# Attention with one query block per head: K of two pairs in 8 KB rows, K and V loaded 64 partitions at a time

## The chip, the cores and the metric

One core of a Trainium2 chip runs the kernel. The metric is device time in microseconds (us); lower is better. A run is called slow when it lies over 1.5% above the fastest of the same kernel.

## The reference

16 batches, 32 query heads, 8 KV heads, 16 queries per head, 2048 keys, head size 128, all in bfloat16. Four query heads share one KV head, so each of the 128 KV heads has 64 query rows.

```python
k = jnp.repeat(k, rep, axis=1); v = jnp.repeat(v, rep, axis=1)      # rep = 4
scores = jnp.einsum("bhqd,bhkd->bhqk", q, k) * D ** -0.5
p = _softmax(scores, axis=-1)
return jnp.einsum("bhqk,bhkd->bhqd", p, v)
```

K and V are 67.1 MB each and are read once. Q and the output are 2.1 MB each.

## The kernel before

A *pair* is two neighbouring KV heads: 128 query rows, one per partition of the scores. The loads fill buffers in SBUF; their rows, 128 here, are called partitions. A load is cut into pieces, here one per partition and row: the prediction calls them descriptors, the trace shows them as packets (32,768 of 4 KB before, 128 for each of the 256 loads of K and V). SyncE (SP) issues all loads and stores in one fixed order, with rings of buffers. Each K or V load is one head, 512 KB, as 128 partitions with 4 KB (16 keys) each:

```python
NBK = 10; NBV = 14; DV = 2; DSTORE = 5          # buffers; V follows K by two pairs, stores by five
...
if kind == "K":
    dst, src = Kn[s][:, :].bitcast(BF16), kf[x].rearrange("(a j) d -> a (j d)", j=J)      # J = 16
elif kind == "V":
    dst, src = Vb[s][:, :, :], vf[x].rearrange("(a j) d -> a j d", j=J)
...
sp.dma_start(dst, src).then_inc(prog.sem_dma[kind][s], 16)
```

VectorE (DVE) transposes K, 1238 ns for a head. TensorE (PE) makes the scores S of a pair (128 by 2048, in PSUM). ScalarE (ACT) takes the exponential, writing P with its columns in another order and summing the rows. PE transposes P, DVE or ACT copies the result out of PSUM, PE multiplies with V, and the result is divided by the row sum and stored:

```python
ins = eng.activation(P[p % 2][:, :].rearrange("m (r a j) -> m a r j", a=4, j=32),
                     src[:, :].rearrange("m (a r j) -> m a r j", a=4, j=32), ACT.Exp, ...,
                     accum_out=rowsum[:, p:p + 1])
```

A second program in the same kernel, with a maximum taken off first, runs only when row sums leave a safe range; with these inputs it does not run.

Of the kernel before, what the change touches and what calls it, by code (L numbers as in the profile page):

```python
# [12 lines left out]
NBK = 10  # L13
NBV = 14
# [3 lines left out]
DV = 2  # L18
# [4 lines left out]
HINT = {"pe": 7, "dve": 10, "act": 3, "pool": 1, "sp": 6}  # L23
# [4 lines left out]
    ("dve", "kx"): 1.25, ("dve", "mx"): 2.38, ("dve", "rc"): 0.17, ("dve", "nm"): 0.36,  # L28
    ("dve", "pe"): 0.69, ("act", "pe"): 1.03, ("act", "qe"): 1.06, ("dve", "qe"): 1.25, ("act", "nm"): 0.42,
    ("act", "ex"): 2.22, ("pool", "qr"): 1.6, ("act", "qr"): 1.1, ("dve", "qr"): 1.1,  # L30
# [6 lines left out]
_SIZE = {"K": 0.524, "V": 0.524, "Q": 0.27, "ST": 0.06}  # L37
_ISSUE = 0.5
_T0 = 1.0
_ENGS = {"kx": ("dve",), "mx": ("dve",), "rc": ("dve",), "nm": ("act", "dve"), "pe": ("act", "dve"),  # L40
         "qe": ("act", "dve"), "qr": ("pool",), "ex": ("act",), "qt": ("pe",), "S": ("pe",), "pt": ("pe",), "pv": ("pe",)}
_PRIO = {"S": 0, "mx": 0, "ex": 0, "pt": 1, "pe": 1, "pv": 2, "rc": 2, "nm": 2, "kx": 3, "qr": 3, "qt": 3, "qe": 3}


def make_ops(NP, pairs_per_chunk, general):

    deps = {}
    dma = []
    ch = lambda p: p // pairs_per_chunk
    n_ch = ch(NP - 1) + 1  # L50
    last_of = lambda c: min(NP, (c + 1) * pairs_per_chunk) - 1

    def add(op, *d):
        deps[op] = [x for x in d if x is not None]

    opt = lambda ok, op: op if ok else None
    for c in range(n_ch):
        add(("Q", c), *[opt(c >= 2, ("qr", c - 2, x)) for x in range(4)])
        for x in range(4):
            prev = ("qe", c, x - 1) if x else opt(c >= 1, ("qe", c - 1, 3))  # L60
            add(("qr", c, x), ("Q", c), opt(c >= 1, ("qt", c - 1, x)))
            add(("qt", c, x), ("qr", c, x), prev)
            add(("qe", c, x), ("qt", c, x), opt(c >= 2, ("S", last_of(c - 2))))
    for g in range(2 * NP):
        p = g // 2
        add(("K", g), opt(g >= NBK, ("kx", g - NBK)))
        add(("V", g), opt(g >= NBV, ("pv", (g - NBV) // 2)))
        add(("kx", g), ("K", g), opt(p >= NKT, ("S", p - NKT)))
    for p in range(NP):
        add(("S", p), ("kx", 2 * p), ("kx", 2 * p + 1), *[("qe", ch(p), x) for x in range(4)],  # L70
            opt(p >= 1, ("mx" if general else "ex", p - 1)))
        if general:
            add(("mx", p), ("S", p), opt(p >= 2, ("ex", p - 2)))
        add(("ex", p), ("mx" if general else "S", p), *[opt(p >= 2, ("pt", p - 2, h)) for h in range(2)])
        for h in range(2):
            add(("pt", p, h), ("ex", p), opt(p >= 1, ("pe", p - 1, h)))
            add(("pe", p, h), ("pt", p, h), opt(p >= NPT, ("pv", p - NPT)))
        add(("pv", p), ("pe", p, 0), ("pe", p, 1), ("V", 2 * p), ("V", 2 * p + 1), opt(p >= 1, ("nm", p - 1)))
        add(("rc", p), ("ex", p))
        add(("nm", p), ("pv", p), ("rc", p), opt(p >= NBO, ("ST", p - NBO)))  # L80
        add(("ST", p), ("nm", p))
    qstep = {max(0, c * pairs_per_chunk - QLEAD): c for c in range(n_ch)}
    dma.append(("Q", 0))
    for t in range(NP + max(DV, DSTORE) + 1):
        if t < NP:
            dma += [("K", 2 * t), ("K", 2 * t + 1)]
        if qstep.get(t, 0):
            dma.append(("Q", qstep[t]))
        if 0 <= t - DV < NP:
            dma += [("V", 2 * (t - DV)), ("V", 2 * (t - DV) + 1)]  # L90
        if 0 <= t - DSTORE < NP:
            dma.append(("ST", t - DSTORE))
    return deps, dma


def pair_of(op, pairs_per_chunk):
    if op[0] in ("qr", "qt", "qe"):
        return op[1] * pairs_per_chunk - 1.5
    return op[1] // 2 if op[0] == "kx" else op[1] + {"S": -1.5, "pv": 1.5}.get(op[0], 0)


def build_schedule(NP, pairs_per_chunk, general):

    deps, dma = make_ops(NP, pairs_per_chunk, general)
    left = sorted((op for op in deps if op[0] in _ENGS),
                  key=lambda op: (pair_of(op, pairs_per_chunk), _PRIO[op[0]]))
    done, free = {}, {"pe": _T0, "dve": _T0, "act": _T0, "pool": _T0, "sp": _T0}
    progs = {"pe": [], "dve": [], "act": [], "pool": [], "sp": []}
    dma_left, dma_end = list(dma), _T0 + _DMA_LAT

    def ready(op):
        r = 0.0
        for d in deps[op]:
            if d not in done:
                return None
            r = max(r, done[d])
        return r

    while left or dma_left:
        best = None  # L120
        if dma_left:
            rd = ready(dma_left[0])
            if rd is not None:
                st = max(free["sp"] + _LAT_SAME, rd + _LAT)
                best = ((round(st, 3), -1, -1), st, "sp", dma_left[0])
        seen = 0
        for op in left:
            rd = ready(op)
            if rd is None:
                continue  # L130
            dur = lambda e: _DUR[op[0]] if e == "pe" else _DUR[(e, op[0])]
            engs = ("dve", "act") if op[:2] == ("qr", 0) else _ENGS[op[0]]
            fin = min((max(free[e] + _LAT_SAME, rd + _LAT) + dur(e), e) for e in engs)
            st = fin[0] - dur(fin[1])
            cand = ((round(st, 3), pair_of(op, pairs_per_chunk), _PRIO[op[0]]), st, fin[1], op)
            if best is None or cand[0] < best[0]:
                best = cand
            seen += 1
            if seen > 40:
                break  # L140
        _, st, eng, op = best
        if eng == "sp":
            dma_left.pop(0)
            end = st + _ISSUE
            dma_end = max(dma_end, end + _DMA_LAT) + _SIZE[op[0]] / _BW
            done[op] = dma_end + (_V_LATE if op[0] == "V" else 0.0)
        else:
            left.remove(op)
            end = st + (_DUR[op[0]] if eng == "pe" else _DUR[(eng, op[0])])
            done[op] = end  # L150
        free[eng] = end
        progs[eng].append(op)
    return deps, progs, max(done.values())


def bass_standalone__gqa_softmax__sampling_kernel(
# [28 lines left out]
    Kn = [sb(f"Kn{i}", [128, J * 64], I32) for i in range(NBK)]  # L185
    KT = [sb(f"KT{i}", [128, 2, J * 64], I32) for i in range(NKT)]
    Vb = [sb(f"Vb{i}", [128, J, 128], BF16) for i in range(NBV)]
    Sneg = [sb(f"Sneg{i}", [128, Sk], F32) for i in range(2)]
# [3 lines left out]
    nbias = sb("nbias", [128, NP], F32)  # L192
    rowsum = sb("rowsum", [128, NP], F32)
    ones = sb("ones", [128, 1], F32)
# [13 lines left out]
    rings = {"K": NBK, "V": NBV, "Q": 2, "ST": NBO}  # L208

    class Program:  # L210
        def __init__(self, tag, general):
            self.general = general
            self.deps, self.progs, _ = build_schedule(NP, qch // 128, general)
            self.sem_eng = {e: sem(f"{tag}_{e}") for e in ("pe", "dve", "act", "pool")}
            self.sem_dma = {kind: [sem(f"{tag}_{kind}{i}") for i in range(n)] for kind, n in rings.items()}
            self.where = {op: (e, i + 1) for e in self.sem_eng for i, op in enumerate(self.progs[e])}

        def point(self, op):
            if op[0] in rings:
                n = rings[op[0]]  # L220
                return self.sem_dma[op[0]][op[1] % n], 16 * (op[1] // n + 1)
# [36 lines left out]
    def elementwise(eng, me, prog, before_last=None):  # L258
        waits = prog.waiter(eng, me)
        for op in prog.progs[me]:  # L260
# [5 lines left out]
            if kind == "kx":  # L266
                ins = eng.transpose(KT[(p // 2) % NKT][:, p % 2, :], Kn[p % NBK][:, :])  # L267
# [5 lines left out]
            elif kind == "mx":  # L273
                ins = eng.tensor_scalar(Sneg[p % 2][:, :], S_ps[:, :], -scale, None,
                                        op0=ALU.mult, op1=ALU.min, accum_out=nbias[:, p:p + 1])
            elif kind == "ex":
                src = Sneg[p % 2] if prog.general else S_ps
                ins = eng.activation(  # L278
                    P[p % 2][:, :].rearrange("m (r a j) -> m a r j", a=4, j=32),
                    src[:, :].rearrange("m (a r j) -> m a r j", a=4, j=32), ACT.Exp,  # L280
                    bias=nbias[:, p:p + 1] if prog.general else 0.0, scale=-1.0 if prog.general else scale,
                    accum_out=rowsum[:, p:p + 1])
# [19 lines left out]
    def transfers(sp, prog):  # L302
        waits = prog.waiter(sp, "sp")
        for op in prog.progs["sp"]:
# [3 lines left out]
            s = x % rings[kind]  # L308
            if kind == "K":
                dst, src = Kn[s][:, :].bitcast(BF16), kf[x].rearrange("(a j) d -> a (j d)", j=J)  # L310
            elif kind == "V":
                dst, src = Vb[s][:, :, :], vf[x].rearrange("(a j) d -> a j d", j=J)
# [6 lines left out]
    def matmuls(pe, prog):  # L319
        waits = prog.waiter(pe, "pe")  # L320
        for op in prog.progs["pe"]:
# [11 lines left out]
            elif kind == "S":  # L333
                c, pp = divmod(p, qch // 128)
                for x in range(4):
                    for a in range(4):
                        for gg in range(2):
# [14 lines left out]
            else:  # L352
                for r in range(J):
                    for gg in range(2):
# [3 lines left out]
                            Vb[(2 * p + gg) % NBV][:, r, :],  # L358
# [20 lines left out]
    with nc.Block() as block:  # L379
# [30 lines left out]
        def _(dve):  # L410
            def count_within():
                dve.wait_ge(*fast.point(("ex", NP - 1)))
# [41 lines left out]
```

## Time and profile before

| | before |
|---|---|
| median (range) | 356.46 us (356.08 to 356.99) |
| span of the profiled run | 353.4 us |
| busy: PE, DVE, ACT | 66%, 68%, 55% |
| bytes moved in the queue of the loads | 138.43 MB |
| rate in the steady part | about 410 GB/s |

The first fence is from the page of the kernel before. The first two rows cut the span into 40 slices: the busy share of the 16 DMA engines in tenths, and the rate in GB/s. Then come the packet count, the chain of work that ended last (shares of the span), DVE's largest group (busy us, mean ns | idle us before it and what ended that), and the two large groups of DMA issues (KB each, median us from issue to landing).

```profile
DMA  7999999999999999999999999999999999999971
GB/s 276 414 408 408 413 408 407 412 413 406 413 408 410 412 410 412 408 413 411 410 411 411 408 412 413 395 411 413 409 411 409 406 413 410 403 409 405 411 287 42
DMA packets 47288, 139.24 MB, mean 394 GB/s; under 512 B 13440, under 2 KB 13440, under 8 KB 47232
DMA 54%; PE 16%; DVE 14%; ACT 7%; SPq 5%; issue 4%
...
L267 DVE STREAM_TRANSPOSE KT<-Kn 128x1024 int32<-128x1024 int32 x128 | 158.1, 1238 | 75.7 <-DMA Kn<-in_k_dram 74.6
...
Kn<-in_k_dram SPq DMA_DIRECT2D x128, 512.0 KB, 12.1
Vb<-in_v_dram SPq DMA_DIRECT2D x128, 512.0 KB, 13.3
```

The DMA engines are full in nearly every slice at about 410 GB/s, and no compute engine is above 68%. DVE's idle time is mostly waiting for K. So the loads bound this kernel, and 138.4 MB at 410 GB/s make 338 of the 353 us.

The end is the other part. These are stretches of the span (start:end and length in us, busy us with instruction counts for PE, its weight loads, DVE, ACT and POOL, then PE clock, DMA share, GB/s).

```profile
330.00:335.00 5.00, 2.77 (x74) 2.07 (x53) 3.02 (x4) 1.97 (x2) 0.00 (x0) 1.00 1.02 409
335.00:340.00 5.00, 3.40 (x102) 2.29 (x104) 4.11 (x7) 3.36 (x4) 0.00 (x0) 1.00 0.94 355
340.00:345.00 5.00, 3.89 (x96) 2.91 (x80) 2.90 (x6) 1.97 (x2) 0.00 (x0) 1.00 0.59 232
```

The rate falls off from 335 us on, while the last loads are still to come.

### The profile page before, as it was taken

The page shows a single profiled execution, that of the slowest core. Times are in us where ns is not written, and L with a number is a line of the kernel's source. Part 1 is how long each engine was busy: PE and PEld are TensorE (multiplying, and loading weights), DVE is VectorE, ACT ScalarE, POOL GpSimd, SP SyncE. Part 2 cuts the span into 40 slices and gives each one's busy share as a digit, 9 for nine tenths or more (in the row PEclk, how much of TensorE's full clock was granted, in tenths as well). Part 3 has the DMA queues.
Part 4 walks back from the last instruction along what each step waited for, and adds up shares of the span by engine and source line. Part 5 has one row for each costly group of instructions (what it writes and reads, how often), then busy time and mean ns, then how long its engine had stood idle before and what let it go on. Part 6 is the DMA issues. An engine that isn't in the chain of part 4 may idle for free.

```text
span 353.4 us, 11937 instructions
## 1 busy us (share of the span) xinstructions
PE 233.8 (66%) x5378; PEld 167.9 (48%) x5378; DVE 239.4 (68%) x340; ACT 193.8 (55%) x214; POOL 28.9 (8%) x35
## 2 busy tenths in 40 slices
PE   2499765776666857756556876676656677566663
PEld 1266543554444634544444655454444545444442
DVE  4668786787685666766766676675776647866761
ACT  6458555754347646665456753576554755554450
POOL 1040000300012000310004000040000400000000
PEclk9999999989999998999999988999999989999997
DMA  7999999999999999999999999999999999999971
GB/s 276 414 408 408 413 408 407 412 413 406 413 408 410 412 410 412 408 413 411 410 411 411 408 412 413 395 411 413 409 411 409 406 413 410 403 409 405 411 287 42
DMA packets 47288, 139.24 MB, mean 394 GB/s; under 512 B 13440, under 2 KB 13440, under 8 KB 47232
## 3 DMA queue, kind: packets, MB, share of 16 engines
q1 hardware_dynamic: 47232, 138.43, 98.7%
q8 instruction: 43, 0.70, 0.8%
q14 instruction: 13, 0.11, 0.1%
HBM read 136.31 MB, written 2.10 MB: 392 GB/s over the span
## 4 chain that ended last, share of the span: by engine, by line
DMA 54%; PE 16%; DVE 14%; ACT 7%; SPq 5%; issue 4%
DMA Kn<-in_k_dram 54%; DVE KT L267 8%; ACT P L278 6%; PE S_ps L340 6%; SPq L317 5%; PE PT_ps L350 5%; PE O_ps L355 5%; DVE PT L299 4%; DVE O L290 1%; PE QT_ps L328 1%; ACT O L288 0%; DVE rrec L284 0%; DVE flag L419 0%
## 5 line engine op out<-in xcount | busy, mean ns | idle before, releaser
L267 DVE STREAM_TRANSPOSE KT<-Kn 128x1024 int32<-128x1024 int32 x128 | 158.1, 1238 | 75.7 <-DMA Kn<-in_k_dram 74.6
L278 ACT ACTIVATE P<-S_ps 128x2048 bf16<-128x2048 f32 x64 | 120.1, 1877 | 78.0 <-PE S_ps L340 77.8
L350 PE MATMUL PT_ps<-ident,P 128*128 128x128 bf16 x1024 | 76.0, 225 | 53.9 <-DVE PT L299 38.3
L340 PE MATMUL S_ps<-KT,QT 32*64 32x512 bf16 x2048 | 74.6, 398 | 45.8 <-DVE KT L267 16.8
L350 PEld LDWEIGHTS PT_ps<-ident,P 128*128 128x128 bf16 x1024 | 60.4, 100 | 77.8 <-issue 40.9
L299 DVE COPY PT<-PT_ps 128x1024 bf16<-128x1024 bf16 x102 | 66.1, 672 | 16.7 <-PE PT_ps L350 16.7
L355 PE MATMUL O_ps<-Vb,PT 128*64 128x128 bf16 x2048 | 73.1, 225 | 6.5 <-issue 5.4
L355 PEld LDWEIGHTS O_ps<-Vb,PT 128*64 128x64 bf16 x2048 | 61.8, 113 | 21.2 <-issue 16.9
L340 PEld LDWEIGHTS S_ps<-KT,QT 32*64 32x64 bf16 x2048 | 28.9, 105 | 69.0 <-DVE KT L267 34.3
L272 POOL COPY Qr<-Qn 128x1024 bf16<-128x1024 bf16 x28 | 27.9, 1041 | 250.4 <-DMA Qn<-in_q_dram 250.4
L288 ACT ACTIVATE O<-O_ps,rrec 128x128 bf16<-128x128 f32 x27 | 9.9, 367 | 56.7 <-PE O_ps L355 56.7
L299 ACT ACTIVATE QT<-QT_ps 128x1024 bf16<-128x1024 bf16 x30 | 30.6, 1019 | 6.6 <-PE QT_ps L328 6.6
L299 ACT ACTIVATE PT<-PT_ps 128x1024 bf16<-128x1024 bf16 x26 | 26.6, 1024 | 5.7 <-PE PT_ps L350 5.7
L328 PE MATMUL QT_ps<-ident,Qr 128*128 128x128 bf16 x256 | 22.4, 238 | 8.4 <-ACT Qr L272 4.5
L328 PEld LDWEIGHTS QT_ps<-ident,Qr 128*128 128x128 bf16 x256 | 17.4, 107 | 12.2 <-issue 7.4
L290 DVE TENSOR_SCALAR O<-O_ps,rrec 128x128 bf16<-128x128 f32 x37 | 12.7, 342 | 7.6 <-PE O_ps L355 7.2
L284 DVE RECIPROCAL rrec<-rowsum 128x1 f32<-128x1 f32 x64 | 9.5, 149 | 4.7 <-ACT P L278 3.8
L278 ACT ACTIVATION_READ_ACCUMULATOR P<-S_ps 128x1 f32 x64 | 12.4, 194 | 0.0
L272 DVE COPY Qr<-Qn 128x1024 bf16<-128x1024 bf16 x2 | 1.3, 690 | 3.3 <-DMA Qn<-in_q_dram 3.3
L299 DVE COPY QT<-QT_ps 128x1024 bf16<-128x1024 bf16 x2 | 2.5, 1225 | 1.2 <-PE QT_ps L328 1.1
L272 ACT ACTIVATE Qr<-Qn 128x1024 bf16<-128x1024 bf16 x2 | 2.0, 1049 | 1.3 <-DMA Qn<-in_q_dram 1.3
L272 ACT ACT_TABLE_LOAD x1 | 1.3, 1283 | 0.7 <-PEq L439 0.7
(12 smaller groups left out, 2.2 us busy)
## 6 DMA issues: line engine op xcount, KB each, us to landing
Kn<-in_k_dram SPq DMA_DIRECT2D x128, 512.0 KB, 12.1
Vb<-in_v_dram SPq DMA_DIRECT2D x128, 512.0 KB, 13.3
Qn<-in_q_dram SPq DMA_DIRECT2D x8, 256.0 KB, 12.0
out_dram<-O SPq DMA_DIRECT2D x64, 32.0 KB, 11.0
```

What stands on the lines that cost most here:

```text
L267: ins = eng.transpose(KT[(p // 2) % NKT][:, p % 2, :], Kn[p % NBK][:, :])
L272: ins = eng.activation(dst, src, ACT.Copy) if me == "act" else eng.tensor_copy(dst, src)
L278: ins = eng.activation(P[p % 2][:, :].rearrange("m (r a j) -> m a r j", a=4, j=32), src[:, :].rearrange("m (a r j) -> m a r j", a=4, j=32) ...
L284: ins = eng.reciprocal(rrec[:, p:p + 1], rowsum[:, p:p + 1])
L288: ins = eng.activation(dst, src, ACT.Copy, scale=r)
L290: ins = eng.tensor_scalar(dst, src, r, None, op0=ALU.mult)
L299: ins = eng.activation(dst, src, ACT.Copy) if me == "act" else eng.tensor_copy(dst, src)
L317: sp.dma_start(dst, src).then_inc(prog.sem_dma[kind][s], 16)
L328: ins = pe.transpose(QT_ps[:, 128 * i:128 * (i + 1)], Qr[:, x, i, :], ident[:, :],)
L340: ins = pe.matmul(S_ps[64 * gg:64 * (gg + 1), 512 * a:512 * (a + 1)], QT[c % 2][32 * a:32 * (a + 1), x, 128 * pp + 64 * gg:128 * pp + 64 * ...
L350: ins = pe.transpose(PT_ps[h][:, 128 * t:128 * (t + 1)], P[p % 2][:, 128 * r:128 * (r + 1)], ident[:, :])
L355: ins = pe.matmul(O_ps[64 * gg:64 * (gg + 1), 0:128], PT[p % NPT][:, r, 64 * gg:64 * (gg + 1)], Vb[(2 * p + gg) % NBV][:, r, :], start=(r ...
```

## The change

The intent: 8 KB descriptors for K in place of 4 KB, and an end in which only V is left to wait for. A K buffer now holds two heads, one on partitions 0 to 63 and one on 64 to 127, with 32 keys (8 KB) per partition. The two heads of a buffer are not neighbours in memory, so each is a load of its own, 64 partitions wide. One block of scores then covers half of the keys of two pairs. As V's rows must match the order of P's columns, V is loaded for both heads of a pair at once, but also in two loads of 64 partitions, each of which takes every second piece of 4 KB. Core of the diff, cuts marked:

```diff
-NBK = 10
-NBV = 14
+NBK = 6
+NBV = 7
-DV = 2
+LAG = 5
 ...
             if kind == "K":
-                dst, src = Kn[s][:, :].bitcast(BF16), kf[x].rearrange("(a j) d -> a (j d)", j=J)
-            elif kind == "V":
-                dst, src = Vb[s][:, :, :], vf[x].rearrange("(a j) d -> a j d", j=J)
+                for pp in range(2):
+                    sp.dma_start(
+                        Kn[s][64 * pp:64 * (pp + 1), :].bitcast(BF16),
+                        kf[4 * (x // 2) + 2 * pp + x % 2].rearrange("(b r) d -> b (r d)", r=2 * J),
+                    ).then_inc(prog.sem_dma[kind][s], 16)
+                continue
+            elif kind[0] == "V":
+                p, part = (x, slice(0, J)) if kind == "V" else (NP - 1, slice(J // 2 * x, J // 2 * (x + 1)))
+                rows = vf[2 * p:2 * p + 2].rearrange("g (b h r) d -> h b g r d", h=2, r=J)
+                for h in range(2):
+                    sp.dma_start(
+                        Vb[p % NBV][64 * h:64 * (h + 1), :, part, :].rearrange("a g r d -> a g (r d)"),
+                        rows[h][:, :, part, :].rearrange("b g r d -> b g (r d)"),
+                    ).then_inc(prog.sem_dma[kind][s], 16)
+                continue
 ...
                 ins = eng.activation(
-                    P[p % 2][:, :].rearrange("m (r a j) -> m a r j", a=4, j=32),
-                    src[:, :].rearrange("m (a r j) -> m a r j", a=4, j=32), ACT.Exp,
+                    P[p % 2][:, :].rearrange("m (r h a j) -> m h a r j", h=2, a=2, j=32)[:, h],
+                    src.rearrange("m (a r j) -> m a r j", a=2, j=32), ACT.Exp,
 ...
```

V now follows K by five pairs and the stores follow V by five; before, both distances were counted from K. The rest of the diff renames the dependencies accordingly, adds up the two half row sums, loads the last V in two parts, and moves the points at which the branch at the end is hinted.

## The prediction

> **What bounds the kernel now.** The DMA queue. Read over stretches from 10 to 330 us, the DMA share is 1.03 at 405 to 412 GB/s. No compute engine comes near: PE 66%, DVE 68%, ACT 55% (busy shares). The chain of waits is 54% K loads, and DVE's largest idle time is 74.6 us of waiting for them. 138.4 MB at 410 GB/s are 338 us of the 353.4 us span. The rest is the start (295 to 385 GB/s up to 8 us) and the end: V's last load is issued only at 336.3 us, because in SP's order it stands behind stores that wait for results; from then the rate falls to 300 to 330 and later 160 to 230 GB/s, so that the last 2.7 MB take 10 us in place of 6.5. The last normalization ends at 348.6 us, the span 4.8 us later.
>
> **What the change does.** Bytes and the number of large loads stay (K 128, V 130). K's descriptors become 8 KB in place of 4 KB, 8192 in place of 16384; V's stay 4 KB. Every K and V load now writes 64 partitions. V follows K by five pairs in place of two, stores follow V by five, and the last V comes in two parts.
> Added: 64 more exponentials (half the size: 1877/2 plus about 0.1 us, plus the 0.194 us accumulator read), about +27 us on ACT in total; 64 additions on DVE at about 0.15 us, +10 us. ACT goes to about 62%, DVE to about 70%. None of this is on the critical path while DMA bounds.
>
> **What lies on the path.**
> 1. The end: K is complete some 12 us before V, the last V is not behind stores, and after it come 0.55 us of PV, 0.36 us of normalization and the store. Gain about 5 us.
> 2. Row size: [...] No run shows it yet.
> 3. The risk: [...] If all engines work in the same half at once the rate could fall far below 410. I expect that the loads of the two halves, queued behind one another some 12 us deep, overlap enough[...]. This is not certain.
>
> **Prediction:** 347 us, range 338 to 366. Faster by over 2%: 0.54, within 2%: 0.28, slower by over 2%: 0.18.
>
> **What would show it.** Right: steady rate 412 to 422 GB/s with a full DMA share; 8192 fewer packets; last V landing about 6 us before the end; a shorter tail of falling rate. Wrong on step 2: rate unchanged at 410 (then about 351 us). Wrong on step 3: rate well under 400 GB/s in all stretches with DMA share full, loads landing later than 13 us.
>
> **What would make it wrong.** [...] V rows that read every second 4 KB being slower from HBM; scores of two pairs waiting for two exponentials, so that loads are issued late and the queue runs dry (DMA share under 1); a longer start, as the first scores need 2 MB in place of 1; or a much better rate from 8 KB rows than estimated.

The sum behind the 347 us: about 356 us before, less 5 for the end, is 351, and the rest, some 4 us, was the row-size term. The 347 us, their range and the steady rate of 412 to 422 GB/s rest on the term too.

## The result, and the profile after

| | before | after |
|---|---|---|
| median (range) | 356.44 us (356.08 to 356.99, 4 runs) | 531.96 us (526.04 to 561.79, 4 runs) |
| ratio of fast runs | | 1.484 (95%: 1.474 to 1.494) |
| span of the profiled run | 353.4 us | 560.0 us (slow) |
| mean granted TensorE clock | 0.97 | 0.73 (0.76 to 0.78 in the fast runs) |

The ratio is the mean time of one kernel's fast runs over that of the other's of the same rounds, so it is not quite the ratio of the medians. Two of the four runs behind the median of the changed kernel are slow ones; its three fast runs took 526.0 to 531.8 us. All its runs together spread by 7%, where the kernel before spreads by 0.3%. The profiled execution of the changed kernel is one of its slow ones, so I read from it only the large effect, which fast runs of simpler kernels confirm below.

The page of the changed kernel, the same views, with the granted PE clock in tenths as first row:

```profile
PEclk9996656877668667785877686677775767678678
DMA  8999999999999999999999999999999999999992
GB/s 200 212 222 223 222 223 230 236 262 273 303 293 347 271 252 253 257 266 272 281 261 256 271 284 291 279 307 232 231 225 232 230 239 247 263 234 236 227 228 75
DMA packets 39382, 139.23 MB, mean 249 GB/s; under 512 B 13472, under 2 KB 13472, under 8 KB 31136
DMA 75%; SPq 8%; PE 7%; DVE 6%; ACT 2%; issue 1%; POOL 0%
...
L287 DVE STREAM_TRANSPOSE KT<-Kn 128x1024 int32<-128x1024 int32 x128 | 154.3, 1229 | 308.0 <-DMA Kn<-in_k_dram 308.0
L306 ACT ACTIVATE P<-S_ps 128x1024 bf16<-128x1024 f32 x128 | 130.4, 1023 | 145.4 <-PE S_ps L382 118.8
...
Kn<-in_k_dram SPq DMA_DIRECT2D x128, 512.0 KB, 21.8
Vb<-in_v_dram SPq DMA_DIRECT2D x126, 512.0 KB, 22.5
```

The DMA share is as full as before. The queue hardly ever runs dry, so the computation does not hold the loads back. The engines are busy and move less: 212 to 223 GB/s in the five slices after the first, about half of 410, and then an uneven 225 to 347. K's waits at DVE went from 75 to 308 us. Loads land 22 us after issue, not 12 to 13. The number of packets fell by 7,906: the 8,192 that the larger rows save, less 256 more pieces of the last V and some 30 small packets. So the layout is as designed.

The trace also records how long each DMA packet took. The medians by packet size:

```
                 256 B    2 KB     4 KB     8 KB
before           18 ns    84 ns   159 ns      -
after            25 ns   144 ns   280 ns   535 ns
```

Packets of every size take longer, including Q's of 2 KB, whose loads did not change (the row after also holds the last V's 2 KB packets; Q's alone took 148 ns). Whatever slows the engines is common to them.

The low PE clock is not the cause: the load-only kernels below lose as much without a single matmul (m_alt took 621 us at a granted clock of 1.00), and the chain of waits runs over K loads and hardly over PE (7%). Whether it is a consequence of PE's waiting is not shown; the traces point that way only in part. In the changed kernel PE paused between matmuls for longer than 3 us 36 times, and up to the last matmul the clock was halved 40 times. In the kernel before it was halved 5 times, though no pause was longer than 2.5 us.

### The profile page after: what moved, and what is told of

It is laid out like the page before. It is cut to its first block, busy times and chain, and to the rows that moved or that the text cites. A ratio compares the mean times of both kernels' runs of the same rounds, so it can differ in the third digit from the quotient of the medians.

```text
span 560.0 us, 12067 instructions
## 1 busy us (share of the span) xinstructions
PE 318.8 (57%) x5378; PEld 229.3 (41%) x5378; DVE 225.3 (40%) x365; ACT 228.6 (41%) x381; POOL 29.0 (5%) x35
## 4 chain that ended last, share of the span: by engine, by line
DMA 75%; SPq 8%; PE 7%; DVE 6%; ACT 2%; issue 1%; POOL 0%
DMA Kn<-in_k_dram 61%; DMA Vb<-in_v_dram 9%; DMA Qn<-in_q_dram 5%; DVE KT L287 5%; SPq L341 4%; SPq L350 3%; PE PT_ps L392 3%; PE S_ps L382 2%; PE O_ps L398 1%; SPq L359 1%; DVE PT L329 1%; ACT PT L329 1%; ACT P L306 1%; PE QT_ps L370 1%; ACT O L318 0%
## 5 line engine op out<-in xcount | busy, mean ns | idle before, releaser
L306 ACT ACTIVATE P<-S_ps 128x1024 bf16<-128x1024 f32 x128 | 130.4, 1023 | 145.4 <-PE S_ps L382 118.8
L392 PE MATMUL PT_ps<-ident,P 128*128 128x128 bf16 x1024 | 104.5, 281 | 104.9 <-DVE PT L329 95.5
L392 PEld LDWEIGHTS PT_ps<-ident,P 128*128 128x128 bf16 x1024 | 89.3, 129 | 136.6 <-issue 93.0
L382 PE MATMUL S_ps<-KT,QT 32*64 32x512 bf16 x2048 | 96.7, 500 | 82.8 <-DVE rowsum L312 56.5
L398 PE MATMUL O_ps<-Vb,PT 128*64 128x128 bf16 x2048 | 100.9, 275 | 25.4 <-DMA Vb<-in_v_dram 24.4
L398 PEld LDWEIGHTS O_ps<-Vb,PT 128*64 128x64 bf16 x2048 | 87.8, 147 | 42.1 <-DMA Vb<-in_v_dram 31.9
L329 ACT ACTIVATE PT<-PT_ps 128x1024 bf16<-128x1024 bf16 x50 | 50.9, 1018 | 15.7 <-PE O_ps L398 10.2
L329 DVE COPY PT<-PT_ps 128x1024 bf16<-128x1024 bf16 x78 | 50.5, 661 | 0.3 <-PE PT_ps L392 0.2
L329 ACT ACTIVATE QT<-QT_ps 128x1024 bf16<-128x1024 bf16 x25 | 25.6, 1023 | 40.6 <-PE QT_ps L370 40.6
L306 ACT ACTIVATION_READ_ACCUMULATOR P<-S_ps 128x1 f32 x128 | 25.5, 199 | 0.0
L312 DVE TENSOR_TENSOR rowsum<-rhalf 128x1 f32<-128x1 f32 x64 | 9.3, 176 | 1.5 <-ACT P L306 1.5
```

The source lines that it names most:

```text
L306: ins = eng.activation(P[p % 2][:, :].rearrange("m (r h a j) -> m h a r j", h=2, a=2, j=32)[:, h], src.rearrange("m (a r j) -> m a r j", a ...
L312: ins = eng.tensor_tensor(rowsum[:, p:p + 1], rhalf[:, p, 0:1], rhalf[:, p, 1:2], op=ALU.add)
L329: ins = eng.activation(dst, src, ACT.Copy) if me == "act" else eng.tensor_copy(dst, src)
L382: ins = pe.matmul(S_ps[64 * gg:64 * (gg + 1), 512 * a:512 * (a + 1)], QT[c % 2][32 * a:32 * (a + 1), x, 128 * pp + 64 * gg:128 * pp + 64 * ...
L392: ins = pe.transpose(PT_ps[h][:, 128 * t:128 * (t + 1)], P[p % 2][:, 128 * r:128 * (r + 1)], ident[:, :])
L398: ins = pe.matmul(O_ps[64 * gg:64 * (gg + 1), 0:128], PT[p % NPT][:, r, 64 * gg:64 * (gg + 1)], Vb[p % NBV][:, gg, r, :], start=(r == 0), ...
```

## The experiments

The theories: **P**, the partitions: a load of 64 partitions that starts at 0 or 64 is slow, about half of the full rate, because of where it lands. **R**: loads of 64 rows, 8 KB rows or V's permuted reading are slow by themselves. **C**: the computation over two pairs holds back the loads. All load-only kernels below give a wrong result (zeros); the kernels with computation are correct. m_low, m_mid, m_twoq, m_mix, b_vhalf and a_vfull were run once each, so only their large differences are read.

### 1. Loads alone, only the first partition changes

A kernel that loads all of K and V once and computes nothing: 256 loads of 64 rows of 8 KB, ten under way. The three runs differ in one expression (written out here; the kernels choose it by a switch):

```diff
 src = (vf if n % 2 else kf)[n // 2].rearrange("(a r) d -> a (r d)", r=32)
-first = 0                # m_low
+first = 32               # m_mid
+first = 64 * (n % 2)     # m_alt
 sp.dma_start(buf[n % 10][first:first + 64, :], src)
```

> Loads only, no compute, wrong result on purpose: 256 loads of 64 rows of 8 KB (134.2 MB), ten under way, all into partitions 0 to 63. Theory P [...]: half of the full rate in every slice, 205 to 225 GB/s, about 620 us. Theory R (64-row loads or 8 KB rows are slow by themselves, wherever they land): about the rate of the changed kernel, 230 to 280 GB/s, 500 to 580 us. Theory C (the changed kernel's loads wait for its computation): 400 GB/s or more, about 340 us.

> The same 256 loads, only the first partition differs: all into partitions 32 to 95, so that each load has 32 partitions of either half. P: the full rate, 400 to 420 GB/s, about 330 to 345 us. R: the same as for partitions 0 to 63, 500 us or more. C: about 340 us here and in the run with partitions 0 to 63.

> The same 256 loads, alternating between partitions 0 to 63 and 64 to 127, as in the changed kernel. P: [...] about 220 GB/s at first; [...] the rate can rise, unevenly, towards 300; 470 to 600 us in all. R: an even 250 GB/s, 500 to 560 us. C: about 340 us.

Measured: m_low 667.6 us, m_mid 331.8 us, m_alt 621.2 us (617.6 and 624.8). The rate rows, m_low first:

```profile
DMA  8999999999999999999999999999999999999997
GB/s 189 207 205 205 205 205 205 205 205 205 205 205 205 205 205 205 205 205 205 205 205 205 205 205 205 205 205 205 205 205 205 205 205 205 205 205 205 205 205 220
```

Then m_mid:

```profile
DMA  7999999999999999999999999999999999999996
GB/s 247 429 423 420 426 419 425 418 424 418 424 420 422 423 420 424 420 425 420 422 420 423 421 422 424 420 425 420 423 419 422 419 424 422 422 420 422 422 406 259
```

Then m_alt:

```profile
DMA  8999999999999999999999999999999999999997
GB/s 198 219 219 218 219 215 220 215 219 218 219 219 219 218 221 217 223 218 222 218 221 218 219 219 219 219 219 219 219 219 219 219 219 219 222 219 220 220 219 234
```

The same bytes in the same number of loads with the same rows take twice as long when the first partition is 0 instead of 32. The median 8 KB packet took 644 ns in m_low and 312 ns in m_mid. Of the three theories only P is left: R expected all three equal and slow, C all three equal and fast. What is shown is that the partitions decide; why they do, the trace does not show. P's sizes were not all right: m_low took 8% more than its 620 us, and m_alt lies above its 470 to 600. m_mid shows that in this run 64 partitions, 8 KB rows and half the rows per load cost nothing when half of the rows lie on either side of partition 64 (331.8 us; 128 partitions with rows of 8 KB took 330.7, experiment 5).

m_alt tests the step on which my prediction rested. Alternating halves gain 7% over one half (219 against 205 GB/s), no more. And my expectation that the rate can rise later, towards 300, fell too: it stays at 219 to the end. The rise to 347 GB/s in the changed kernel's (slow) profiled run would then come with what m_alt lacks, among it the 128-partition loads of Q and the stores; I did not test that.

### 2. An attempt to start one group of engines later

```diff
+sp.dma_start(extra[64:72, :], kf[0][0:256].rearrange("(a r) d -> a (r d)", r=32))   # 8 partitions, before all loads
```

> As the alternating run, with one 64 KB load in front that has only 8 partitions (64 to 71, 8 KB each)[...]. P, [...] the rate starts near 400 GB/s in place of 220; total 335 to 450 us[...]. [...] R and C: no difference from the alternating run.

P had a second branch, no difference from the alternating run.

Measured: 628.7 us (627.2 and 630.2), 212 to 221 GB/s in the slices: no gain over m_alt. But the edit did not do what it was meant to. In the trace the extra load is eight packets of about 0.4 us, over by 2.2 us, and the first large load's packets begin only at 2.5 us: no engine started late. So this run tests nothing about a start apart.

### 3. The two halves from two queues

The lower halves are issued by SP and the upper halves by ACT, five under way each.

```diff
-for n in range(loads):               # all from SP
+for n in range(0, loads, 2):         # SP: partitions 0 to 63
+for n in range(1, loads, 2):         # ACT: partitions 64 to 127
```

> The alternating load-only run (wrong result on purpose), with the loads into partitions 0 to 63 issued by SP and those into 64 to 127 by ACT, five under way on each queue. [...] 330 to 420 GB/s, 330 to 420 us. [...] 219 GB/s, about 620 us, as in the alternating run.

These are the two outcomes that P left open.

Measured: 510.4 us. Neither outcome came. The rate rows and the two queues (packets, MB, share of the 16 engines):

```profile
GB/s 202 251 249 249 251 251 251 249 251 251 249 251 251 249 249 252 250 251 249 251 250 250 251 256 261 276 284 298 298 301 307 304 309 309 309 306 310 309 310 268
...
q1 hardware_dynamic: 10384, 69.21, 50.7%
q10 hardware_dynamic: 10240, 67.12, 49.8%
```

Two queues give 250 and later 310 GB/s, so part of the loss hangs on both halves standing in one queue. They do not bring back the 422 of m_mid. What changed at slice 25 the trace does not show.

### 4. Half loads in the kernel before, and whole V loads in the changed kernel

b_vhalf is the kernel before with only V's loads cut at partition 64:

```diff
-sp.dma_start(Vb[s][:, :, :], rows)
+for part in (slice(0, 64), slice(64, 128)):
+    sp.dma_start(Vb[s][part, :, :], rows[part])
```

> The kernel before, with each V load cut into two loads of 64 partitions (0 to 63, then 64 to 127); rows of 4 KB, addresses, order and computation as before. P: V's half of the bytes goes at 220 to 300 GB/s, K's at 410; about 400 to 480 us. R (8 KB rows, or reading every second 4 KB of V) and C: no change, 354 to 360 us.

a_vfull is the changed kernel with V on 128 partitions; the exponential writes P's columns in the natural order of the keys instead:

```diff
-P[p % 2][:, :].rearrange("m (r h a j) -> m h a r j", h=2, a=2, j=32)[:, h],
+P[p % 2][:, :].rearrange("m (r a j h) -> m h a r j", h=2, a=2, j=32)[:, h],
...
-rows = vf[2 * p:2 * p + 2].rearrange("g (b h r) d -> h b g r d", h=2, r=J)       # two loads of 64 partitions
+rows = vf[2 * p + gg].rearrange("(a r) d -> a r d", r=J)                          # two loads of 128
```

> The changed kernel, with V in loads of 128 partitions again (two per pair, rows of 4 KB in natural order; the exponentials write the columns of P in the matching order, so the result is right); K stays in halves. P: K's half of the bytes stays slow, V's is fast: 400 to 480 us. If V's permuted rows were the cause: about 345 to 355 us. If K's half loads or the computation over two pairs were the whole cause: no change, 525 to 560 us.

Measured: b_vhalf 590.2 us, a_vfull 580.7 us, one run each, both correct. b_vhalf shows in the real kernel that cutting loads at partition 64 is enough for the damage: its bytes, rows, addresses and computation are those of before. (It also has 256 V loads of 256 KB in place of 128 of 512 KB; the changed kernel has no such smaller loads but for the last V, so their number is not what slows that one.) But both are slower than the 400 to 480 us that I expected of one slow half of the bytes. They are also above the changed kernel, in which both K and V are cut, though by only 3 to 5% against its slowest run. The rate row of b_vhalf, and then that of a_vfull:

```profile
GB/s 297 283 270 260 251 254 256 256 259 243 245 241 242 237 243 248 241 233 230 228 223 223 225 227 231 222 226 231 234 233 224 226 235 231 233 239 239 246 227 74
```

```profile
GB/s 203 221 246 254 262 273 255 249 259 267 260 239 252 258 244 235 225 228 234 236 240 236 236 236 238 235 253 246 241 238 234 235 235 237 240 238 236 239 271 154
```

In a_vfull the packets tell the two kinds of load apart: K's halves have 8 KB packets, V's whole loads 4 KB. The 4 KB packets took 282 ns in the median, against 159 ns before. So whole loads slow down too when half loads are among them.

m_mix has the loads of b_vhalf without any computation, in another order and with ten under way. The loads, in words:

```diff
+if n % 3 == 0:  K of head n // 3 on 128 partitions, rows of 4 KB
+else:           V of head n // 3, partitions 64 * (n % 3 - 1) to + 63, rows of 4 KB
```

> Loads only (wrong result on purpose): the loads of b_vhalf, K on 128 partitions, V in halves of 256 KB, rows of 4 KB, ten under way, nothing computed. If each kind of load keeps its own rate (410 GB/s full, 219 GB/s half), the two halves of the bytes take 164 and 306 us: about 480 us, an even 285 GB/s. If [...] full loads slow down as well: 550 to 600 us as in b_vhalf, with a rate that begins near 285 and falls. If b_vhalf's excess came from its computation, this run stays at 480 us or under.

Measured: 536.3 us.

```profile
GB/s 227 256 268 258 259 272 257 257 256 249 244 246 247 246 254 252 250 251 254 260 255 254 261 258 259 264 262 260 264 259 257 259 260 255 254 255 257 254 254 241
```

The loads alone lose more than the sum of their parts: 67.1 MB at 410 and 67.1 MB at 219 GB/s would take 164 and 306 us, 470 together. (219 was measured with 8 KB rows, here they are 4 KB.) But 536 us lies in neither of the expected ranges, and the rate is about 255 from the start and does not begin at 285 and fall, so the falling rate that I expected is not confirmed. Why whole loads slow down among half loads is not shown. The 54 us between m_mix and b_vhalf are not explained either.

### 5. What 8 KB rows are worth

m_full4 loads 256 times 128 partitions by 4 KB, m_full8 128 times 128 partitions by 8 KB (two heads next to each other in memory).

> Loads only (wrong result on purpose): 256 loads of 128 partitions with rows of 4 KB, the loads of the kernel before, ten under way. All theories: about 410 GB/s, 335 to 345 us. It is the base for the 8 KB rows.

> Loads only (wrong result on purpose): 128 loads of 128 partitions with rows of 8 KB, 1 MB each, six under way. P: full rate; whether 8 KB rows are worth 1 to 3% as the prediction had it (415 to 422 GB/s) or nothing is what this run tells. R (8 KB rows are slow): under 300 GB/s, over 450 us.

Measured: 340.3 us (340.2 to 340.5) and 330.7 us (330.5 to 330.9); in their middle slices 409 to 410 and 416 to 427 GB/s. 8 KB rows are 2.8% faster. Their median packet took 313 ns; two of 4 KB took 324. Theory R's "8 KB rows are slow" is refuted.

### 6. The change with loads on all 128 partitions

If pairs are heads 4s and 4s+2, and 4s+1 and 4s+3, the two heads in a K buffer are neighbours in memory. Then 128 rows of 8 KB are one contiguous 1 MB, and one load does it. f_full8 has this, V as in a_vfull, and each store in two, as the heads of a pair are no longer neighbours:

```diff
-for pp in range(2):
-    sp.dma_start(Kn[s][64 * pp:64 * (pp + 1), :].bitcast(BF16),
-                 kf[4 * (x // 2) + 2 * pp + x % 2].rearrange("(b r) d -> b (r d)", r=2 * J))
+dst = Kn[s][:, :].bitcast(BF16)
+src = kl[2 * Sk * x:2 * Sk * (x + 1), :].rearrange("(b r) d -> b (r d)", r=2 * J)    # kl: rows of all heads
...
-c, pp = divmod(2 * (p // 2) + a // 2, qch // 128)        # columns 128*pp + 64*gg of Q^T
+c, hh = divmod(4 * (p // 2) + 2 * gg + a // 2, qch // 64)    # columns 64*hh
```

> The changed kernel with every K and V load on 128 partitions: a K load holds two neighbouring heads (1 MB, 128 rows of 8 KB, one piece of memory), pairs become heads 4s and 4s+2, 4s+1 and 4s+3; V natural, rows of 4 KB; each store in two. P: the loss is gone, and what the prediction expected of 8 KB rows and of the earlier V comes: steady rate 414 to 418 GB/s, 342 to 349 us. If the interleaved computation or the later V cost anything by themselves, it stays above 356 us.

f_full4 is the same with a gap in the K buffer between the two halves of a row, so that the descriptors are 4 KB (`Kn` of 2 by 1040 words in place of 2048):

> As f_full8, but K's rows land in two pieces of 4 KB each with a gap between them, so that K's descriptors are 4 KB again; all else equal. From the load-only runs (410 against 422 GB/s) K's half of the bytes should lose about 2.9%, 4 to 6 us of the whole, so about 349 to 353 us. If the row size does not matter in the kernel: equal to f_full8 within 0.3%.

f_lag2 is f_full8 with `LAG = 2` in place of 5:

> As f_full8, but V follows K by two pairs, as in the kernel before, in place of five. If the later V shortens the end as predicted, this is 2 to 6 us slower than f_full8; if not, equal within 0.3%.

| kernel | median us (range of fast runs) | ratio to before (95%) |
|---|---|---|
| f_full8 | 351.1 (350.7 to 351.3) | 0.986 (0.983 to 0.988) |
| f_full4 | 353.5 (353.0 to 353.8) | 0.992 (0.990 to 0.994) |
| f_lag2 | 357.7 (355.9 to 358.4) | 1.003 (1.000 to 1.006) |

The interleaved scores, the longer lag and the 8 KB rows are all still in f_full8, and the 175 us are gone. Only the load shapes were changed, with what they entail. f_full8's page: rates, packets and the exponentials.

```profile
GB/s 314 423 414 411 415 409 415 413 411 417 414 416 413 416 416 416 412 415 416 415 415 415 415 410 418 411 416 416 413 416 411 414 415 417 411 421 411 386 295 51
DMA packets 39383, 139.24 MB, mean 399 GB/s; under 512 B 13472, under 2 KB 13472, under 8 KB 31136
...
L307 ACT ACTIVATE P<-S_ps 128x1024 bf16<-128x1024 f32 x128 | 164.7, 1306 | 40.0 <-PE S_ps L383 33.7
```

The steady rate is 414 to 415 GB/s, within what was predicted. The 8 KB rows of K are worth 2.4 us (f_full4 less f_full8), half of what I expected; f_full4 came out 0.5 us above its range. The exponentials that write P with a stride take 1306 ns in place of the changed kernel's 1023, and ACT is 73% busy. The loads stay full (DMA share 1.02 to 1.03 from 4 to 320 us), but the exponentials are 14% of the chain of waits, and no run tells what they cost.

Within this layout the longer lag, which moves the stores too, is worth 6.6 us (f_lag2 less f_full8), a little over the expected 2 to 6. But f_lag2 is 1.6 us slower than the kernel before of the same rounds (356.1), in spite of its 8 KB rows: at a lag of two pairs the new layout itself costs some 4 us (an estimate: 1.6 and the 2.4 of the rows), and part of the 6.6 only takes that back. In f_lag2 the rate holds at 414 GB/s a slice less and then ends in a long tail, in which the computation of the last pairs is left to do:

```profile
GB/s 316 415 415 416 412 411 414 413 414 418 414 414 413 415 416 414 416 416 413 414 417 416 412 414 415 413 414 414 418 409 417 414 415 414 417 415 414 310 68 17
```

### 7. Why f_full8 is not faster still

f_full8 missed its own expectation (342 to 349) by 2 us. Its end, as stretches:

```profile
325.00:330.00 5.00, 3.39 (x84) 2.29 (x84) 3.27 (x7) 2.67 (x5) 0.00 (x0) 1.00 0.99 370
330.00:335.00 5.00, 4.10 (x113) 3.12 (x112) 1.72 (x6) 4.60 (x6) 0.00 (x0) 1.00 1.00 378
335.00:340.00 5.00, 3.40 (x83) 2.74 (x80) 2.64 (x7) 1.28 (x3) 0.00 (x0) 1.00 0.64 236
340.00:345.00 5.00, 2.48 (x66) 1.99 (x66) 1.03 (x7) 0.00 (x0) 0.00 (x0) 1.00 0.26 75
```

The last V load was issued at 332.2 us. f_more has more buffers (`NBK = 7`, `NBV = 9`); f_store8 has besides `DSTORE = 8` and 12 output tiles.

> f_full8 with one more K buffer and two more V buffers (7 and 9), so that the last V loads are issued earlier. In f_full8 the rate falls to 370 GB/s from 325 us on and its last V load was issued at 332 us. If the V ring held those loads back: 1 to 4 us faster than f_full8's 351.1. If it was the order of waits in SP or the engines' uneven ends: equal within 0.3%.

> f_more with each store issued eight pairs behind its V in place of five (12 output tiles), so that the last V loads stand behind older stores. If stores that wait for results hold the last V loads back: V's last load before 330 us and 1 to 3 us faster than f_more's 350.3. If the end is long because the engines finish unevenly what is queued: equal within 0.3%.

Measured: f_more 350.3 us (350.0 to 351.0; ratio 0.983, 0.981 to 0.984), f_store8 350.8 us (350.1 to 351.4; ratio 0.984, 0.981 to 0.986). In both the last V load was still issued at about 332 us, and the end looks the same. So neither the size of the V ring nor the distance of the stores is what makes it long. The profile of f_full8 shows what the time is: from 335 us on every load has been issued, yet a third of the engines' time, and later three quarters, is idle while PE waits for the last V (it came at 343.2 us). Finer stretches show how:

```profile
334.00:336.00 2.00, 1.39 (x22) 1.24 (x23) 1.77 (x6) 1.26 (x3) 0.00 (x0) 1.00 1.00 377
336.00:338.00 2.00, 1.97 (x50) 1.60 (x48) 0.71 (x5) 0.66 (x1) 0.00 (x0) 1.00 0.55 210
338.00:340.00 2.00, 0.97 (x32) 0.81 (x30) 0.93 (x2) 0.36 (x1) 0.00 (x0) 1.00 0.55 202
340.00:342.00 2.00, 1.08 (x32) 0.92 (x32) 0.36 (x2) 0.00 (x0) 0.00 (x0) 1.00 0.51 159
```

The DMA share drops to about a half at once and stays there for 6 us. The share is a mean over 16 engines: whether about half of them were done while the others still worked, the trace does not tell, and why the share falls is open. f_more is the fastest correct kernel, 1.7% under the kernel before, and within some 0.3% of f_full8.

## Why the prediction was wrong, point by point

- **That the DMA queue bounds the kernel: right.** Therefore everything hung on its rate.
- **Step 3, the risk: this step failed, and with it the number.** The prediction said "I expect that the loads of the two halves, queued behind one another some 12 us deep, overlap enough". The runs show 219 GB/s for alternating halves against 205 for one half and 422 for the same loads at partition 32. With ten loads under way, alternating gave 7%; the overlap that the step counted on did not come beyond that. No run had measured it then; I had put an argument in the place of one. The drawn-out end of the trace, on which I leaned, was no evidence of overlap: m_alt stays at 219 GB/s to its end.
- **The chances.** 0.18 for "slower" and an upper bound of 366 us were wrong even for someone unsure: the two outcomes of step 3 lay far apart. Half the rate on all K and V bytes would have been 134 MB at 205 GB/s, some 650 us: an estimate, from the 410 GB/s of the profile before. The load-only m_alt took 621 us, m_low 668. A range up to 366 left out the bad case altogether.
- **Step 2, 8 KB rows: the direction was right, the size was over-estimated for the kernel.** The forecast's sum counted some 4 us (351 less 347); measured 2.4 us in the kernel (f_full4 against f_full8). With all bytes in 8 KB rows and nothing computed it is 2.8%, which would be some 4.6 us on K's half; why the kernel gets only half of that was not tested. In the change itself it could not show.
- **Step 1, the end: the direction was right, the size about half.** Predicted 5 us. f_full4 has the new end and layout but 4 KB rows, and gains 2.6 us over the kernel before of the same rounds (356.1 less 353.5). The 6.6 us of LAG 5 against 2 look like a hit, but part of them pays for the new layout. Against the kernel before all of the change's good parts came to 5.0 us (356.1 less 351.1), not the 9 predicted. How much of the rest the DMA's end at half its share took is not shown.
- **The added computation: right that it does not bind in the steady part.** The changed kernel's ACT is at 41% and DVE at 40% of its span with the DMA share full, and in f_full8 the whole interleaved scheme runs within 351 us (ACT 73%, DVE 65%; predicted 62% and 70%). An added exponential, over 1024 columns, took 1023 ns in the changed kernel and 1306 ns in f_full8; one over 2048 took 1877 ns before. At the end it can bind: with a lag of two pairs it is what f_lag2 still has to do when its loads are over.
- **What would show step 3 wrong** was named rightly: a rate well under 400 with the DMA share full, and landings later than 13 us. That is what the profile showed: 249 GB/s in the mean, and 22 us.

## What to carry to other kernels

Look at which partitions each load covers, not only at its bytes and rows: 64 partitions from 32 to 95 loaded at 422 GB/s, and 64 from 0 or alternating from 0 and 64 at about half of that. A busy DMA share does not tell a good load from a bad one; bytes per second and the time of a packet do. If a layout needs two heads side by side on the partitions, choose heads that are neighbours in memory, so that one load covers all 128, and let another engine with time to spare (here the exponential's write order) put the columns right (1306 ns for an exponential in f_full8, against 1023 in the changed kernel); and when a prediction hinges on one uncertain step, let the range hold both of its outcomes.
